# Banded attention and an ELU feed-forward layer on one core: rows of q and k spread by twos over 32 partitions

## The chip, the cores and the metric

The kernel runs on one NeuronCore of a Trainium2 chip, in one launch. The metric is the device time of a launch in microseconds. A core has five engines with a queue each, which work through their instructions in order and wait for each other through semaphores: TensorE (PE, matrix products), VectorE (DVE), ScalarE (ACT), GpSimd (POOL) and SyncE (SP, which here only issues DMAs). [...] All DMAs run on the same 16 DMA engines.

## The reference

```python
# q, k, v: [8 batches, 8 heads, 576, 64] float32; w_in [512, 2048], w_out [2048, 512]
scores = (q @ k.T) / sqrt(64)
rel    = i - j                                   # query row minus key row
mask   = (rel >= 0) & (rel < 128)
scores = where(mask, scores - slope[head] * abs(rel), -1e9)      # slope = 2 ** -(head + 1)
attn   = exp(scores - max) / sum
x      = (attn @ v) as [4608 tokens, 512]
h      = x @ w_in
out    = where(h > 0, h, exp(min(h, 0)) - 1) @ w_out             # [4608, 512] float32
```

A query row sees at most 128 keys, so that of the 576 x 576 scores of a head only a band is computed.

## The kernel before

**Layout of the attention.** A batch has 8 heads in four groups g of two, h2 = 0 and 1; group g has the partitions 32g to 32g+31. TensorE needs q and k with the 64 values of a row on the partitions, as two halves dh of 32. They come there in two steps. `load_qk(b, w, g)` (line 67) is a DMA of POOL that fetches two heads of q (w = 0) or k (w = 1), turns float32 into float16 and spreads the 576 rows over 32 partitions: partition i gets the 18 adjacent rows 18i to 18i+17 (R = 18), which lie behind one another in DRAM, 4,608 bytes a head. `turn_qk(b, w, h2, dh)` (line 74) then transposes on VectorE, in blocks of 32 x 32: for each r it takes 32 partitions by 32 values and writes a row of 32 values, one for each i, to the columns 18i + r of `QT` or `KT`. Its writes are thus 18 float16 values, 36 bytes, apart. A batch takes 8 loads and 8 transposes of 576 values per partition.

**The rest of the attention.** `scores` (line 145) multiplies on TensorE into one PSUM tile `sp`, four head groups side by side. ScalarE takes the exponential (`expo`, line 159), VectorE multiplies by a table `TAB` of bias and mask (`weigh`, line 162), TensorE multiplies by v with a column of ones (`values`, line 173; its PSUM tile `av` has one buffer), VectorE divides by the sum (line 188, 189). v comes by SP's DMAs (`load_v`, line 78, five tiles `vf`), and POOL casts it into `VP` (`cast_v`, line 83). `turn` brings the result to `xT`: by a DMA transpose, or for batch 0 by TensorE.

**The feed-forward layer** takes tokens in 9 blocks of 512, 16 steps each. `hidden` (line 213) makes a 128 x 512 tile `hp` on TensorE (two buffers), ScalarE takes its exponential into `e`, POOL clips it to at most 1, and `elu` (line 230) puts both together on VectorE into `g`, which frees `hp`. `output` (line 238) multiplies four chunks of `g` by `w_out`; after four such steps ScalarE copies the sum and SP stores it.

**The order of the work** is written out by hand, in slots (lines 257 to 357). A slot s issues, in this order: the early tasks (`before`, the exponentials), `hidden` of s, `elu` of s - 1, the tasks of `at(s, ...)`, `output`. Each engine takes its instructions in this order. Batch b > 0 starts at slot a = START[b] = 5, 21, 37, 55, 73, 91, 109: its loads are issued in the slots a-12 to a-5, one each (those of batch 1 before slot -5), its v loads from a-6 (batch 1: a-4), its transposes in a-4 to a+3, one each, its scores in a, a+4, a+8, a+12. Slots with a negative number are batch 0's first half, ahead of the first `hidden`. The transposes of batches 2 to 7 thus begin in the slots 17, 33, 51, 69, 87 and 105.

**The start.** POOL issues the 8 loads of batch 0, an iota for the table, the four weight loads `wi`, the 8 loads of batch 1, then the casts of v of batch 0. Its DMAs take turns on eight semaphores, so that an issue waits until the DMA eight places ahead of it has landed. SP issues v of batch 0 at once. `warm` (line 252) is a row of products of `ident` into a tile that nobody reads.

Of the kernel before, what the change touches and what calls it, by code (L numbers as in the profile page):

```python
# [7 lines left out]
F32 = mybir.dt.float32  # L8
F16 = mybir.dt.float16
# [9 lines left out]
def kernel(  # L19
# [9 lines left out]
    nc = tc.nc  # L29
    B, H, S, D = q.shape  # L30
    NTOK, DO = out.shape
# [2 lines left out]
    NTB = NTOK // 512  # L34
    RING = 3 * S
    VW = D + 2
    R = S // 32
    V = nc.vector

    const = ctx.enter_context(tc.tile_pool(name="const", bufs=1))  # L40
    stage = ctx.enter_context(tc.tile_pool(name="stage", bufs=2))
# [5 lines left out]
    ps_o = ctx.enter_context(tc.tile_pool(name="ps_o", bufs=1, space=PSUM))  # L47

    def one(shape, dt, name):
        return const.tile(shape, dt, name=name, tag=name)  # L50
# [5 lines left out]
    QT = [one([128, 2, 2, S], F16, f"QT{i}") for i in range(2)]  # L56
    KT = [one([128, 2, 2, 640], F16, f"KT{i}") for i in range(2)]
# [7 lines left out]
    st, vf = {}, {}  # L65

    def load_qk(b, w, g):
        if b not in st:
            st[b] = stage.tile([128, 2, 2, R, D], F16, name="st")
        nc.gpsimd.dma_start(  # L70
            st[b][32 * g:32 * g + 32, w, :, :, :].rearrange("p h r d -> p h (r d)"),
            (q, k)[w][b, 2 * g:2 * g + 2, :, :].rearrange("h (i r) d -> i h (r d)", r=R))

    def turn_qk(b, w, h2, dh):
        o = (QT, KT)[w][b % 2][:, h2, dh, 0:S].rearrange("p (i r) -> p r i", r=R)
        V.transpose(o, st[b][:, w, h2, :, 32 * dh:32 * dh + 32])  # L76

    def load_v(b, n):
        t = vf[b, n] = stage.tile([128, H, D], F32, name="vf", tag="vf", bufs=5)
        p = 128 if n < 4 else 64  # L80
        nc.sync.dma_start(t[0:p, :, :], v[b, :, 128 * n:128 * n + p, :].rearrange("h p d -> p h d"))

    def cast_v(b, n):
# [5 lines left out]
    def load_wi(i, n=1):  # L89
        c = slice(512 * i, 512 * i + 512 * n)  # L90
        nc.gpsimd.dma_start(w_in_sb[:, :, c], moe_w_in[:, c].rearrange("(c p) f -> p c f", p=128))
# [8 lines left out]
    with tc.manual_schedule():  # L100
# [7 lines left out]
        for g in range(4):  # L108
            load_qk(0, 1, g)
            load_qk(0, 0, g)  # L110
        for c, n in ((0, 256), (256, 192), (448, 64)):
            nc.gpsimd.iota(rel[:, c:c + n], pattern=[[1, n]], base=0, channel_multiplier=-1)
        load_wi(0)
        load_wi(1)
        for n in range(5):
            load_v(0, n)

        rowf = one([128, 1], F32, "rowf")
        V.tensor_copy(rowf, row)
# [127 lines left out]
                nc.scalar.copy(ob, ops[t])  # L247
                nc.sync.dma_start(out[512 * t + 128 * ts:512 * t + 128 * ts + 128, :], ob)

        spare = ps_o.tile([128, DO], F32, name="spare", tag="op")  # L250

        def warm(n):
            for _ in range(n):
                nc.tensor.matmul(spare[:, 0:128], ident, ident, start=True, stop=True)

# [3 lines left out]
        def at(s, f, *a):  # L259
            tasks.setdefault(s, []).append((f, a))  # L260
# [7 lines left out]
        START = [None, 5, 21, 37, 55, 73, 91, 109]  # L268


        warm(60)
        for h2 in range(2):
            for w in (1, 0):
                for dh in range(2):
                    at(-5 + h2, turn_qk, 0, w, h2, dh)
# [38 lines left out]
        for b in range(1, B):  # L314
            a = START[b]
            for k_ in range(4):
                u, h2 = divmod(k_, 2)
                at(a + 4 * k_, scores, b, k_)
                for g in range(4):
                    before(a + 4 * k_ + 1 + g, expo, b, k_, g)  # L320
                for gp in range(2):
                    at(a + 4 * k_ + 2 + 2 * gp, weigh, b, k_, gp)
                for n, i in enumerate((0, 1) if u == 0 else (2, 3, 4)):
                    at(a + 4 * k_ + 5 + n, values, b, i, h2)
                    if h2:
                        at(a + 4 * k_ + 5 + n, turn, b, i)
            order = [(w, h2, dh) for h2 in range(2) for w in (1, 0) for dh in range(2)]
            for n, what in enumerate(order):
                at(a - 4 + n, turn_qk, b, *what)
            for n in range(5):  # L330
                at(a - 6 + n if b > 1 else a - 4 + n, load_v, b, n)
                at(a - 2 + n, cast_v, b, n)
            if b > 1:
                for g in range(4):
                    for w in range(2):
                        at(a - 12 + 2 * g + w, load_qk, b, 1 - w, g)
# [51 lines left out]
```

## Time and profile before

| | us |
|---|---|
| median of 3 runs (lowest, highest) | 463.75 (462.43, 465.34) |
| the profiled execution, its own time | 464.51 |
| its span, first to last instruction | 462.2 |
| PE busy, share of the span | 338.5, 73% |
| DVE busy | 346.7, 75% |
| ACT busy | 176.9, 38% |
| POOL busy | 155.6, 34% |
| mean granted clock of TensorE | 0.882 |

A row of a group gives the line of the code, the engine, the operation and its tiles (out<-in), shapes as partitions x elements, the count; then busy time in us, the mean of one in ns, and how long the engine sat idle just before, with what ended the wait. [...] Busy times of engines overlap; those of one engine's instructions can overlap a little too.

### The profile page before, as it was taken

The page shows a single profiled execution, that of the slowest core. Times are in us where ns is not written, and L with a number is a line of the kernel's source. Part 1 is how long each engine was busy: PE and PEld are TensorE (multiplying, and loading weights), DVE is VectorE, ACT ScalarE, POOL GpSimd, SP SyncE. Part 2 cuts the span into 40 slices and gives each one's busy share as a digit, 9 for nine tenths or more (in the row PEclk, how much of TensorE's full clock was granted, in tenths as well). Part 3 has the DMA queues.
Part 4 walks back from the last instruction along what each step waited for, and adds up shares of the span by engine and source line. Part 5 has one row for each costly group of instructions (what it writes and reads, how often), then busy time and mean ns, then how long its engine had stood idle before and what let it go on. Part 6 is the DMA issues. An engine that isn't in the chain of part 4 may idle for free.

```text
span 462.2 us, 8158 instructions
## 1 busy us (share of the span) xinstructions
PE 338.5 (73%) x3280; PEld 226.8 (49%) x3280; DVE 346.7 (75%) x453; ACT 176.9 (38%) x317; POOL 155.6 (34%) x265
## 2 busy tenths in 40 slices
PE   4017467756697669987699468966698569999996
PEld 4006456533365345654366335643465346676652
DVE  3995998769867995699857997699867995674340
ACT  3122322513254234532256234533264234544441
POOL 7220532504143332523245223523263331333330
PEclk9555765979799797988889999999999897999999
DMA  9990750771249011961039211951069110211101
GB/s 172 199 208 1 107 90 13 90 151 34 54 81 181 23 28 37 143 144 24 29 62 186 62 42 35 155 131 28 24 115 183 40 36 7 64 45 53 47 23 68
DMA packets 69317, 37.16 MB, mean 80 GB/s; under 512 B 56480, under 2 KB 60576, under 8 KB 69280
## 3 DMA queue, kind: packets, MB, share of 16 engines
q0 software_dynamic: 9344, 13.64, 21.5%
q1 hardware_dynamic: 59936, 23.01, 19.7%
q8 instruction: 25, 0.41, 0.4%
q14 instruction: 12, 0.10, 0.1%
HBM read 36.70 MB, written 9.44 MB: 100 GB/s over the span
## 4 chain that ended last, share of the span: by engine, by line
DVE 44%; PE 37%; DMA 9%; issue 5%; ACT 3%; POOL 2%; DVEq 0%; ACTq 0%; POOLq 0%
PE op L243 18%; DVE QT L76 17%; PE hp L222 15%; DVE KT L76 14%; DMA st<-in_k_dram 7%; DVE g L234 6%; DVE EX L171 3%; DVE xn L189 3%; PE sp L154 3%; PE av L183 2%; DMA st<-in_q_dram 2%; ACT EX L160 1%; DVE rden L188 1%; ACT e L226 1%; POOL e L227 1%
## 5 line engine op out<-in xcount | busy, mean ns | idle before, releaser
L222 PE MATMUL hp<-xT,wi 128*128 128x256 f16 (+3 forms) x1408 | 163.7, 269 | 57.7 <-DVE g L234 57.7
L227 POOL TENSOR_SCALAR e<-e 128x512 f32<-128x512 f32 x144 | 90.9, 631 | 274.5 <-ACT e L226 274.5
L222 PEld LDWEIGHTS <-wi 128*128 128x128 f16 x1408 | 129.4, 106 | 109.0 <-issue 68.1
L226 ACT ACTIVATE e<-hp 128x512 f32<-128x512 f32 x144 | 86.1, 598 | 198.9 <-PE hp L222 198.9
L243 PE MATMUL op<-wo,g 128*128 128x512 f16 x576 | 157.3, 400 | 1.4 <-ACT ob L247 1.4
L234 DVE SCALAR_TENSOR_TENSOR g<-e,hp 128x512 f16<-128x512 f32 x144 | 108.5, 753 | 53.0 <-POOL e L227 53.0
L160 ACT ACTIVATE EX<-sp 128x512 f16<-128x512 f32 x128 | 75.2, 598 | 51.0 <-PE sp L154 50.7
L76 DVE STREAM_TRANSPOSE KT<-st 128x576 f16<-128x576 f16 x32 | 84.4, 2660 | 10.5 <-DMA st<-in_k_dram 10.3
L76 DVE STREAM_TRANSPOSE QT<-st 128x576 f16<-128x576 f16 x32 | 84.3, 2655 | 0.0
L243 PEld LDWEIGHTS <-g 128*128 128x128 f16 x576 | 51.3, 101 | 47.8 <-issue 13.1
L154 PE MATMUL sp<-QT,KT 32*128 32x256 f16 (+2 forms) x640 | 27.0, 284 | 48.1 <-DVE QT L76 43.4
L171 DVE TENSOR_TENSOR EX<-EX,TAB 128x1024 f16<-128x1024 f16 x64 | 48.1, 754 | 1.1 <-ACT EX L160 0.9
L154 PEld LDWEIGHTS <-KT 32*128 32x128 f16 x640 | 15.6, 99 | 57.7 <-issue 40.4
L183 PE MATMUL av<-VP,EX 128*128 128x65 f16 x576 | 33.7, 202 | 9.8 <-DVE xn L189 8.0
L188 DVE RECIPROCAL rden<-av 128x4 f32<-128x4 f32 x80 | 14.6, 182 | 30.1 <-PE av L183 29.2
L183 PEld LDWEIGHTS <-EX 128*128 128x128 f16 x576 | 29.8, 104 | 13.4 <-issue 5.2
L189 DVE TENSOR_TENSOR xn<-av,rden 128x256 f16<-128x256 f32 x80 | 34.0, 425 | 2.8
L247 ACT COPY ob<-op 128x512 f32<-128x512 f32 x36 | 21.1, 585 | 24.8 <-PE op L243 24.8
L85 POOL TENSOR_SCALAR VP<-vf 128x512 f16<-128x512 f32 (+1 forms) x40 | 24.5, 615 | 6.2 <-DMA vf<-in_v_dram 6.2
L70 POOL DMA_DIRECT2D st<-in_k_dram x32 | 18.3, 571 | 5.8 <-DMA wi<-in_moe_w_in_dram 5.1
L70 POOL DMA_DIRECT2D st<-in_q_dram x32 | 18.0, 563 | 5.3 <-DMA wi<-in_moe_w_in_dram 4.8
L135 ACT ACTIVATE TAB<-ra 128x512 f16<-128x512 f32 x8 | 4.3, 614 | 7.0 <-DVE ra L132 7.0
(25 smaller groups left out, 30.0 us busy)
## 6 DMA issues: line engine op xcount, KB each, us to landing
out_dram<-ob SPq DMA_DIRECT2D x36, 256.0 KB, 2.2
vf<-in_v_dram SPq DMA_DIRECT2D x32, 256.0 KB, 5.4
st<-in_k_dram POOLq DMA_DIRECT2D x32, 144.0 KB, 4.7
st<-in_q_dram POOLq DMA_DIRECT2D x32, 144.0 KB, 4.2
wi<-in_moe_w_in_dram POOLq DMA_DIRECT2D x4, 512.0 KB, 12.8
wo<-in_moe_w_out_dram POOLq DMA_DIRECT2D x4, 512.0 KB, 6.1
vf<-in_v_dram SPq DMA_DIRECT2D x8, 128.0 KB, 4.4
xT<-xn SPq DMA_TRANSPOSE x35, 2.4
```

What stands on the lines that cost most here:

```text
L70: nc.gpsimd.dma_start(st[b][32 * g:32 * g + 32, w, :, :, :].rearrange("p h r d -> p h (r d)"), (q, k)[w][b, 2 * g:2 * g + 2, :, :].rearran ...
L76: V.transpose(o, st[b][:, w, h2, :, 32 * dh:32 * dh + 32])
L154: nc.tensor.matmul(sp[:, g, o:o + n], kt[r, h2, dh, 128 * kb:128 * kb + 128], qt[r, h2, dh, q0:q0 + n], start=dh == 0, stop=dh == 1, tile_ ...
L160: nc.scalar.activation(unit(b, k_)[:, g, 0:512], sp[:, g, :], AF.Exp, scale=0.125)
L171: V.tensor_tensor(out=e, in0=e, in1=t, op=ALU.mult)
L183: nc.tensor.matmul(a[:, g, :], e[:, g, c:c + 128], VP[b % 2][:, n, 2 * g + h2, 0:D + 1], start=j == 0, stop=j == len(parts) - 1)
L189: V.tensor_tensor(out=xnt[b, i][:, :, h2, :], in0=a[:, :, 0:D], in1=r.unsqueeze(2).broadcast_to([128, 4, D]), op=ALU.mult)
L222: nc.tensor.matmul(p[:, l * w + u0:l * w + u1], w_in_sb[:, c, fc * 128:(fc + 1) * 128], xT[:, c, x0:x0 + u1 - u0], start=(c == 0), stop=(c ...
L226: nc.scalar.activation(e, p, AF.Exp)
L227: nc.gpsimd.tensor_scalar(out=e, in0=e, scalar1=1.0, scalar2=0.0, op0=ALU.min, op1=ALU.max)
L234: V.scalar_tensor_tensor(out=gs[t][:, f0:f0 + nf, c0:c0 + w], in0=sh(es.pop((t, j))), scalar=1.0, in1=sh(hps.pop((t, j))), op0=ALU.subtrac ...
L243: nc.tensor.matmul(ops[t], gs[t][:, fc, ts * 128:(ts + 1) * 128], w_out_sb[:, fc, :], start=(fc == 0), stop=(fc == NFC - 1))
```

## The change

- Row s of a head is now 64n + 2i + j, with n = 0 to 8, i = 0 to 31 and j = 0, 1: partition i gets rows by twos, nine pairs that lie 64 rows apart. A load moves 576 pieces of 512 bytes instead of 64 of 4,608.
- A transposed row of 32 values, one for each i, is written to the columns 64n + 2i + j: every 4 bytes instead of every 36. What is read, the number of transposes and their size stay.
- For batch 0, POOL writes one column of each v tile before SP may load it; in the code this stands behind the first weight load, and the second weight load follows it.
- `warm` takes a PSUM buffer of its own at each call, has 100 products instead of 60 at the beginning, and three more calls with 30 each in the slots -5, -4 and -3.

```diff
--- before.py
+++ after.py
@@ -34,7 +34,7 @@
     NTB = NTOK // 512
     RING = 3 * S
     VW = D + 2
-    R = S // 32
+    R = S // 64
     V = nc.vector
 
     const = ctx.enter_context(tc.tile_pool(name="const", bufs=1))
@@ -66,18 +66,20 @@
 
     def load_qk(b, w, g):
         if b not in st:
-            st[b] = stage.tile([128, 2, 2, R, D], F16, name="st")
+            st[b] = stage.tile([128, 2, 2, R, 2, D], F16, name="st")
         nc.gpsimd.dma_start(
-            st[b][32 * g:32 * g + 32, w, :, :, :].rearrange("p h r d -> p h (r d)"),
-            (q, k)[w][b, 2 * g:2 * g + 2, :, :].rearrange("h (i r) d -> i h (r d)", r=R))
+            st[b][32 * g:32 * g + 32, w, :, :, :, :].rearrange("p h n j d -> p (h n) (j d)"),
+            (q, k)[w][b, 2 * g:2 * g + 2, :, :].rearrange("h (n i j) d -> i (h n) (j d)", i=32, j=2))
 
     def turn_qk(b, w, h2, dh):
-        o = (QT, KT)[w][b % 2][:, h2, dh, 0:S].rearrange("p (i r) -> p r i", r=R)
-        V.transpose(o, st[b][:, w, h2, :, 32 * dh:32 * dh + 32])
+        o = (QT, KT)[w][b % 2][:, h2, dh, 0:S].rearrange("p (n i j) -> p n j i", i=32, j=2)
+        V.transpose(o, st[b][:, w, h2, :, :, 32 * dh:32 * dh + 32])
 
     def load_v(b, n):
         t = vf[b, n] = stage.tile([128, H, D], F32, name="vf", tag="vf", bufs=5)
         p = 128 if n < 4 else 64
+        if b == 0:
+            nc.gpsimd.memset(t[:, 0, 0:1], 0.0)
         nc.sync.dma_start(t[0:p, :, :], v[b, :, 128 * n:128 * n + p, :].rearrange("h p d -> p h d"))
 
     def cast_v(b, n):
@@ -111,9 +113,9 @@
         for c, n in ((0, 256), (256, 192), (448, 64)):
             nc.gpsimd.iota(rel[:, c:c + n], pattern=[[1, n]], base=0, channel_multiplier=-1)
         load_wi(0)
-        load_wi(1)
         for n in range(5):
             load_v(0, n)
+        load_wi(1)
 
         rowf = one([128, 1], F32, "rowf")
         V.tensor_copy(rowf, row)
@@ -247,9 +249,8 @@
                 nc.scalar.copy(ob, ops[t])
                 nc.sync.dma_start(out[512 * t + 128 * ts:512 * t + 128 * ts + 128, :], ob)
 
-        spare = ps_o.tile([128, DO], F32, name="spare", tag="op")
-
         def warm(n):
+            spare = ps_o.tile([128, DO], F32, name="spare", tag="op")
             for _ in range(n):
                 nc.tensor.matmul(spare[:, 0:128], ident, ident, start=True, stop=True)
 
@@ -268,7 +269,10 @@
         START = [None, 5, 21, 37, 55, 73, 91, 109]
 
 
-        warm(60)
+        warm(100)
+        at(-5, warm, 30)
+        at(-4, warm, 30)
+        at(-3, warm, 30)
         for h2 in range(2):
             for w in (1, 0):
                 for dh in range(2):
```

On POOL, at the start, where the loads of batch 0 end and the weights begin (`st` is the staged q or k, `wi` the first weight matrix, the numbers after DMASW one of POOL's eight semaphores). Before:

```order
L70 DMA st<-in_k_dram 32x2x1152
L70 DMA st<-in_q_dram 32x2x1152
L112 IOTA rel 128x256
L112 IOTA rel 128x192
L112 IOTA rel 128x64
L91 DMA wi<-in_moe_w_in_dram 128x4x512 [waits DMASW0_49]
L91 DMA wi<-in_moe_w_in_dram 128x4x512 [waits DMASW1_49]
```

And now:

```order
L70 DMA st<-in_k_dram 32x18x128
L70 DMA st<-in_q_dram 32x18x128
L114 IOTA rel 128x256
L114 IOTA rel 128x192
L114 IOTA rel 128x64
L93 DMA wi<-in_moe_w_in_dram 128x4x512 [waits DMASW0_49]
L82 MEMSET vf 128x1 x5
L93 DMA wi<-in_moe_w_in_dram 128x4x512 [waits DMASW1_49]
```

Five memsets have come between the first and the second weight load; the loads of q and k stand where they stood, in another shape.

Further on in POOL's queue, the last loads of batch 1 and the casts of batch 0's v (`vf` into `VP`), now:

```order
L70 DMA st<-in_k_dram 32x18x128 [waits DMASW2_49]
L70 DMA st<-in_q_dram 32x18x128 [waits DMASW3_49]
L87 TENSOR_SCALAR VP_85<-vf 128x8x64 [waits DMAHW0_49,Pool_49]
L87 TENSOR_SCALAR VP_85<-vf 128x8x64 [waits DMAHW1_49,Pool_49]
L87 TENSOR_SCALAR VP_85<-vf 128x8x64 [waits DMAHW2_49,Pool_49]
```

The casts still stand behind all of batch 1's loads, and these still wait for the weight loads; nothing has moved here.

On SP, the loads of v of batch 0, now:

```order
L83 DMA vf<-in_v_dram 128x8x64 [waits Pool_49] x4
L83 DMA vf<-in_v_dram 64x8x64 [waits Pool_49]
```

They stand first in SP's queue as before, where they waited for nothing; now they wait for POOL's memsets.

## Rows read from the trace of the kernel before

**Rows 1.** The page, busy time and its share of the span, by engine
```profile
PE 338.5 (73%) x3280; PEld 226.8 (49%) x3280; DVE 346.7 (75%) x453; ACT 176.9 (38%) x317; POOL 155.6 (34%) x265
```

**Rows 2.** The page, the chain that ended last, by engine and by line
```profile
DVE 44%; PE 37%; DMA 9%; issue 5%; ACT 3%; POOL 2%; DVEq 0%; ACTq 0%; POOLq 0%
PE op L243 18%; DVE QT L76 17%; PE hp L222 15%; DVE KT L76 14%; DMA st<-in_k_dram 7%; DVE g L234 6%; DVE EX L171 3%; DVE xn L189 3%; PE sp L154 3%; PE av L183 2%; DMA st<-in_q_dram 2%; ACT EX L160 1%; DVE rden L188 1%; ACT e L226 1%; POOL e L227 1%
```

**Rows 3.** Stretch, length, then busy PE, PEld, DVE, ACT, POOL, granted clock, DMA share, GB/s
```profile
40.50:96.10 55.60, 37.89 (x503) 31.39 (x500) 43.32 (x58) 21.93 (x40) 20.52 (x34) 0.74 0.51 71
96.10:353.60 257.50, 198.37 (x1884) 127.92 (x1885) 211.03 (x270) 104.16 (x189) 91.12 (x151) 0.92 0.43 82
252.50:281.00 28.50, 16.39 (x154) 10.17 (x153) 28.30 (x27) 8.81 (x16) 8.21 (x14) 1.00 0.25 67
281.00:303.00 22.00, 21.31 (x219) 14.89 (x218) 14.58 (x28) 12.35 (x23) 10.30 (x18) 1.00 0.71 118
353.60:382.00 28.40, 17.10 (x195) 10.88 (x191) 28.19 (x27) 8.49 (x15) 7.79 (x13) 0.91 0.24 65
400.00:462.20 62.20, 56.78 (x429) 36.53 (x426) 24.96 (x43) 24.00 (x42) 16.61 (x28) 1.00 0.14 48
```

**Rows 4.** Groups by line in 252.5 to 281: busy us, mean ns | idle before
```profile
L76 DVE STREAM_TRANSPOSE KT<-st 128x576 f16<-128x576 f16 x4 | 10.6, 2643 | 0.1
L234 DVE SCALAR_TENSOR_TENSOR g<-e,hp 128x512 f16<-128x512 f32 x8 | 7.0, 872 | 0.0
L171 DVE TENSOR_TENSOR EX<-EX,TAB 128x1024 f16<-128x1024 f16 x3 | 2.0, 661 | 0.0
L189 DVE TENSOR_TENSOR xn<-av,rden 128x256 f16<-128x256 f32 x4 | 1.7, 425 | 0.1
L188 DVE RECIPROCAL rden<-av 128x4 f32<-128x4 f32 x4 | 0.7, 168 | 0.0
```

**Rows 5.** Groups by line and form, whole run: the transposes, two DVE rows, POOL's DMA issues
```profile
L76 DVE STREAM_TRANSPOSE KT<-st 128x576 f16<-128x576 f16 x32 | 84.4, 2660 | 10.5 <-DMA st<-in_k_dram 10.3
L129 DVE TENSOR_TENSOR ra<-ra,rel 128x512 f32<-128x512 f32 x1 | 0.7, 693 | 0.0
L123 DVE MEMSET VP<- 128x40 f16 x2 | 0.2, 92 | 0.2
L70 POOL DMA_DIRECT2D st<-in_k_dram x32 | 18.3, 571 | 5.8 <-DMA wi<-in_moe_w_in_dram 5.1 <-DMA st<-in_k_dram 0.3 <-issue 0.3
L91 POOL DMA_DIRECT2D wi<-in_moe_w_in_dram x4 | 3.0, 750 | 1.5 <-DMA st<-in_k_dram 1.0 <-DMA st<-in_q_dram 0.4
```

**Rows 6.** Timeline of the start: start, length, engine, line, idle before
```profile
1.62 5.09 PE L254 MATMUL spare<-ident 128*128 128x128 f16 x60 [1.62 <-DVE ident L120]
12.61 5.10 DVE L76 STREAM_TRANSPOSE KT<-st 128x576 f16<-128x576 f16 x2 [3.65 <-DMA st<-in_k_dram]
25.57 0.53 POOL L70 DMA_DIRECT2D st<-in_q_dram  x1 [1.99 <-DMA wi<-in_moe_w_in_dram]
26.13 2.36 POOL L85 TENSOR_SCALAR VP<-vf 128x512 f16<-128x512 f32 x4
33.30 0.64 PE L183 MATMUL av<-VP,EX 128*128 128x65 f16 x4
40.52 1.91 PE L222 MATMUL hp<-xT,wi 128*128 128x128 f16 x16
```

**Rows 7.** The page, DMA queues over the run: packets, MB, share of 16 engines
```profile
q0 software_dynamic: 9344, 13.64, 21.5%
```

**Rows 8.** DMA queues in 0 to 12: packets, MB, share of 16 engines
```profile
q1 hardware_dynamic: 3505, 0.89, 35.1%
```

**Rows 9.** DMA queues in 80 to 90
```profile
q0 software_dynamic: 335, 0.62, 48.9%
```

**Rows 10.** DMA queues in 42 to 60
```profile
q0 software_dynamic: 1450, 1.45, 55.6%
```

**Rows 11.** Timeline of VectorE where batch 2's first transpose starts
```profile
96.11 2.64 DVE L76 STREAM_TRANSPOSE KT<-st 128x576 f16<-128x576 f16 x1 [3.52 <-DMA st<-in_k_dram]
```

## The prediction

> **What bounds the kernel now.** I read the page's totals first, then the chain of waits, then busy time by stretch, then the groups of one stretch. In the totals no engine is full: VectorE has 75% and TensorE 73% [rows 1]. The chain says that the two take turns: VectorE carries 44% of it, TensorE 37%, and the lines that stand out are the two transposes of line 76 with 31% together [rows 2]. The stretches show the turns. From 252.5 to 281 us, the eight slots in which batch 5's q and k are transposed, VectorE is busy for 28.30 of 28.5 us and TensorE for 16.39. From 281 to 303, the next ten slots, TensorE is busy for 21.31 of 22 us and VectorE for 14.58 [rows 3]. So a batch costs about 28.5 + 22 = 50.5 us, the first part set by VectorE and the second by TensorE. In the first part the eight transposes hold 21.1 us (four of k at 10.6, four of q alike), the rest 11.4 us of durations: g 7.0, weighing 2.0, xn 1.7, reciprocals 0.7 [rows 4]. These records overlap a little, since 28.30 is less than their sum; without the transposes VectorE has between 28.30 - 21.1 = 7.2 and 11.4 us to do there. The last 62.2 us hold no transposes [rows 3].
>
> **The transposes.** 64 of them, 2.66 us for 576 values per partition [rows 5], 4.6 ns a value. The input is read in the same runs of 32 values; only the step of the writes changes, from 36 bytes to 4. No transpose with another step is in this trace. The bounds come from other VectorE rows. Below: line 129 writes one 4-byte value after another, so every 4 bytes, at 693 ns for 512 values [rows 5], 1.35 ns each; 576 of these are 0.78 us. Above, if a small step helps at all: the memset of line 123 writes 40 values 132 bytes apart in 92 ns [rows 5], 2.3 ns each or 1.32 us for 576; and if the step does not matter, the 2.66 us stay. I take 0.78, because line 129 is the row with exactly the new step. The memset speaks against me in part: its writes lie further apart than today's transposed ones and cost half as much, so the step alone may not explain 4.6 ns.
>
> [...]
>
> **What that is worth, stage by stage** (462.2 us of span, 464.5 as timed in the profiled execution; the median is 463.75, 0.75 less).
> - *Batches 2 to 6, 96.1 to 353.6 us*, 88 slots, 257.5 us [rows 3]. The eight transposing slots: VectorE has 7.2 to 11.4 us plus 8 x 0.78 = 6.2, so 13.4 to 17.6; TensorE has its 16.39. The two come level; I take 18 us instead of 28.5. The other ten slots stay at 22, since TensorE fills them. That makes 40 us for a batch of 18 slots; one of the five has 16 slots, two of the 2-us kind fewer, 36. Sum 4 x 40 + 36 = 196, **61.5 us less**.
> - *Batch 7's transposes*, 28.4 us with VectorE busy for 28.19 [rows 3]: 18 instead, **10.4 less**. The 80 us behind them I leave as they are.
> - *Batch 1, 40.5 to 96.1*, 55.6 us: VectorE is busy for 43.32 and would be for 43.3 - 8 x 1.88 = 28.3. [...] I take 38, TensorE's own time, **17.6 less**.
> - *The start, 0 to 40.5.* Batch 0's eight transposes run from 12.61 to about 32.5, the first values at 33.30, the first hidden product at 40.52 [rows 6]. Eight short ones would be done by 19 us, 13 us earlier. But the values also need VP, and POOL casts v at 26.13, right after the last of its load issues, which sat behind a landing weight load until 25.57 [rows 6]. That order stays, so only 33.3 - 26.7 = 6.6 us can be had. Of this the smaller packets (below) take up to 3.3 us, for twelve loads ahead of the cast; I keep **5 less**.
>
> **The loads of q and k.** 64 loads go from 64 packets of 4,608 bytes to 576 of 512 bytes. *On POOL*: an issue of 64 packets takes 571 ns, one of 512 takes 750 [rows 5], 0.4 ns a packet, so 0.2 us more each, 13 us in all. POOL is busy for 34% [rows 1], and each slot of 2 us holds one issue and one 0.6-us operation on e: hidden by POOL's idle time. Were POOL full, it would be 13 us. *On the DMA engines*: the queue's 9,344 packets [rows 7] are 64 x 64 + 8 x 512 of data and 1,152 others, 16 for each DMA. In 80 to 90 us it carried q and k alone, 335 packets in 48.9% of 160 engine-us [rows 9], 234 ns a packet, or 292 for each data packet if the small ones are free. By bytes 512 of them cost 32 ns. The v loads' packets of 256 bytes cost 35.1% of 192 engine-us over 3,505, 19 ns [rows 8]; the weights' of 2,048 cost 55.6% of 288 over 1,450, 110 ns [rows 10]. So a new packet lies between 19 and 110 ns. I take 40, near the byte rate and twice the v packet: 576 x 40 / 16 engines = 1.44 us a load against 1.17. One load is issued per slot of 2.2 us, so they still fit; twelve at the start add 3.3 us, taken off above. The first transpose of a batch already waits for its k load now and then, 3.52 us at the worst [rows 11]; 0.3 us more of that is inside my rounding of 17.6 to 18.
>
> [...]
>
> **The small edits, together.** v of batch 0 now waits for POOL's memsets, five of about 0.1 us, behind the first weight load. It leaves the engines to q and k in the first 9 us, which may bring the first transpose forward by 2 us, off the path since the cast decides. v then has from 9 to 29 us to land; if it were later than that, the start would grow by what it is late. The added products of ident: 60 took 5.09 us [rows 6], so 130 end near 12.7 us, before the first transposes are done; the two later sets of 30, 2.5 to 5 us each, stand in the stretch in which TensorE waits for the cast. Cost nothing; without that cover, 10 us.
>
> **Sum**: -61.5 - 10.4 - 17.6 - 5 = -94.5. 464.5 - 94.5 = 370.0, by the median **369 us**.
>
> **Rivals.**
> 1. *Transposes of 1.32 us*, the memset's price. For it: that row is a write with a step. Against: its step is 132 bytes. A transposing stretch has 17.8 to 22 us of VectorE, I take 21: 3 more, six times, and 4 in batch 1: **391 us**. Chance 0.14.
> 2. *Packets at twice the byte rate*, 64 ns: 2.3 us a load, a little over a slot. Each of six batches is late by 8 x 0.1 us, and the start by 8 x 1.1: **383**. Chance 0.07.
> 3. *The step does not set the price*: transposes stay at 2.66 us. For it the memset row, against it nothing in the trace. VectorE bounds the same stretches, the start gains at most 2 us and loses 1: **463**. Chance 0.09.
> 4. *Slower: a packet costs what a weight packet does*, 110 ns, whatever its bytes. A load then takes 4.0 us, and the eight are issued 2.2 us apart; the first transposes of six batches come 8 x 1.8 = 14 us late and the start 8 x 2.8 = 22 later, 108 in all. With the gain this is 477; it decides from about 104 ns, where 48 x (0.036 p - 2.2) + 8 x (0.036 p - 1.17) eats up 94.5. Against it: 19 ns for 256 bytes. Time **477**, chance 0.04.
>
> **The numbers.** The forecast has 0.66. Its own range is 345 to 385: below, if the eight slots run at TensorE's 16.4 (10 us), batch 1 takes 32 at a better clock (6), the start gives all 6.6 (1.6), and batches 2 to 6, at a mean clock of 0.92 [rows 3], win back half of 0.08 x 198 (8); above, at 2.5 us more per transposing stretch. With rivals 1 and 2 the range is 345 to 398 and holds 0.66 x 0.9 + 0.14 + 0.07 = 0.8. A measurement of this kernel can tell about 1%. Faster by more: 0.66 + 0.14 + 0.07 = 0.87. Within 1%: rival 3, 0.09. Slower: 0.04.
>
> **What would show it.** The transpose rows at 0.7 to 0.9 us; at 1.3 rival 1 is right, at 2.6 rival 3. TensorE above 88% of the span, and its waits for g in the transposing slots nearly gone. The first values near 29 us, behind the cast of v. The q0 packets: 42,112, at about 40 ns. I am wrong if the idle time before the first transpose of each batch grows to several us (the loads), if the hidden products still wait for g although VectorE is not full (the way from hidden product through ScalarE and POOL back to VectorE being too long), or if the cast of v slips past 33 us.

## The result, and the profile after

The changed kernel takes **353.08 us** (median of 4 runs, 352.23 to 353.57) against 464.54 (4 runs, 462.43 to 466.15): a ratio of 0.760, with an interval of 0.756 to 0.764. Forecast were 369 us, with a range of 345 to 398. The span of the profiled execution went from 462.2 to 350.9 us, 111.3 less, where the sum had 94.5. Slow executions, among them ones of 553, 824 and 1,241 us, are left out of the ratios.

Line numbers of the kernel after are two higher than before from line 81 on, and four at the end. First the page of the kernel after: the totals, the chain by engine, and POOL's DMA queue. They answer to [rows 1, 2, 7].

```profile
PE 314.4 (90%) x3410; PEld 221.1 (63%) x3410; DVE 236.6 (67%) x453; ACT 176.3 (50%) x317; POOL 169.6 (48%) x270
PE 71%; DVE 8%; DMA 8%; issue 4%; ACT 4%; POOL 3%; ACTq 0%; DVEq 0%; POOLq 0%
q0 software_dynamic: 42112, 13.64, 36.6%
```

VectorE's share of the chain has fallen from 44% to 8%, TensorE's has grown from 37% to 71%, and TensorE is busy for 90% of the span. The queue has the 42,112 packets that were worked out. Their price: 36.6% of 350.9 us on 16 engines are 2,055 engine-us; less 4,096 weight packets at the 110 ns that they took in the kernel before [rows 10], 1,604 remain for 36,864 packets, 44 ns each (forecast: 40).

The groups by line and form over the whole run, to set beside [rows 5], and the start, to set beside [rows 6] (start, length, engine, line, idle before):

```profile
L76 DVE STREAM_TRANSPOSE KT<-st 128x576 f16<-128x576 f16 x32 | 25.9, 817 | 3.4 <-DMA st<-in_k_dram 3.3
L70 POOL DMA_DIRECT2D st<-in_k_dram x32 | 22.1, 690 | 6.1 <-DMA wi<-in_moe_w_in_dram 5.6 <-issue 0.5
```

```profile
1.62 10.22 PE L255 MATMUL spare<-ident 128*128 128x128 f16 x130 [1.62 <-DVE ident L122]
11.16 1.50 DVE L76 STREAM_TRANSPOSE KT<-st 128x576 f16<-128x576 f16 x2 [0.94 <-DMA st<-in_k_dram]
26.31 0.66 POOL L70 DMA_DIRECT2D st<-in_q_dram  x1 [2.70 <-DMA wi<-in_moe_w_in_dram]
26.99 1.21 POOL L87 TENSOR_SCALAR VP<-vf 128x512 f16<-128x512 f32 x2
27.68 0.38 PE L185 MATMUL av<-VP,EX 128*128 128x65 f16 x4 [8.54 <-POOL VP L87]
34.89 1.91 PE L224 MATMUL hp<-xT,wi 128*128 128x128 f16 x16
```

A transpose takes 0.82 us instead of 2.66, forecast were 0.78. An issue on POOL has grown from 571 to 690 ns, 0.12 us instead of the 0.2 that were allowed. At the start the transposes run from 11.16 us, but the values wait for the cast of v, which stands behind the last load issue as it did: first values at 27.68 instead of 33.30, first hidden product at 34.89 instead of 40.52.

Busy time by stretch, in the columns of [rows 3]: batch 1; batches 2 to 6; the eight transposing slots of batch 5 and the ten slots behind them; batch 7's transposing slots; the rest.

```profile
34.90:73.90 39.00, 30.27 (x496) 24.63 (x495) 29.32 (x59) 21.02 (x39) 22.32 (x34) 0.92 0.88 124
73.90:257.90 184.00, 179.05 (x1886) 122.19 (x1883) 142.59 (x271) 104.58 (x190) 100.14 (x151) 1.00 0.71 116
183.60:198.40 14.80, 14.29 (x138) 9.64 (x139) 13.95 (x27) 8.05 (x15) 7.85 (x13) 1.00 0.46 104
198.40:221.40 23.00, 22.31 (x239) 15.46 (x238) 15.14 (x28) 13.00 (x24) 11.84 (x19) 1.00 0.81 126
257.90:272.50 14.60, 14.44 (x184) 10.50 (x183) 13.69 (x26) 7.80 (x15) 8.10 (x13) 1.00 0.47 109
272.50:350.90 78.40, 72.43 (x600) 47.45 (x599) 35.42 (x63) 33.24 (x59) 21.48 (x35) 1.00 0.16 49
```

Transposing slots and the others now look alike. In the eight slots from 183.6 us both engines are nearly full, TensorE for 14.29 and VectorE for 13.95 of 14.8 us; in the ten behind them TensorE is, for 22.31 of 23.0. The granted clock, a share of full speed, had a mean of 0.74 in batch 1 and 0.92 in batches 2 to 6 [rows 3]; now it is 0.92 and then 1.00. The groups of those eight slots answer to [rows 4]. First TensorE's groups in the same slots before, which [rows 4] does not have, and then now:

```profile
L222 PE MATMUL hp<-xT,wi 128*128 128x256 f16 x60 | 7.8, 272 | 9.2 <-DVE g L234 9.2
L243 PE MATMUL op<-wo,g 128*128 128x512 f16 x30 | 7.8, 380 | 0.0
L154 PE MATMUL sp<-QT,KT 32*128 32x256 f16 x32 | 1.6, 272 | 2.9 <-DVE QT L76 2.9
```

```profile
L224 PE MATMUL hp<-xT,wi 128*128 128x256 f16 x58 | 7.6, 272 | 0.2 <-DVE g L236 0.2
L245 PE MATMUL op<-wo,g 128*128 128x512 f16 x28 | 7.2, 379 | 0.0
L156 PE MATMUL sp<-QT,KT 32*128 32x256 f16 x20 | 0.9, 271 | 0.3 <-ACT EX L162 0.3
L236 DVE SCALAR_TENSOR_TENSOR g<-e,hp 128x512 f16<-128x512 f32 x8 | 5.2, 653 | 0.3 <-POOL e L229 0.3
L76 DVE STREAM_TRANSPOSE KT<-st 128x576 f16<-128x576 f16 x4 | 3.3, 822 | 0.3 <-DMA st<-in_k_dram 0.3
L173 DVE TENSOR_TENSOR EX<-EX,TAB 128x1024 f16<-128x1024 f16 x3 | 2.0, 679 | 0.0
L191 DVE TENSOR_TENSOR xn<-av,rden 128x256 f16<-128x256 f32 x4 | 1.7, 425 | 0.1
L190 DVE RECIPROCAL rden<-av 128x4 f32<-128x4 f32 x4 | 0.7, 172 | 0.4 <-PE av L185 0.4
```

TensorE hardly waits for g any longer: 0.2 us of idle time ahead of the hidden products instead of 9.2. g itself has become shorter, 653 ns instead of 872; why was not tried. A product takes as long as before, but fewer of them fall into these slots: 58, 28 and 20 here, where 60, 30 and 32 stood.

| stretch | before, us | after, us | less by | forecast |
|---|---|---|---|---|
| start, to the first hidden product | 40.5 | 34.9 | 5.6 | 5 |
| batch 1, to batch 2's first transpose | 55.6 | 39.0 | 16.6 | 17.6 |
| batches 2 to 6 | 257.5 | 184.0 | 73.5 | 61.5 |
| batch 7's transposing slots | 28.4 | 14.6 | 13.8 | 10.4 |
| the rest | 80.2 | 78.4 | 1.8 | 0 |

### The profile page after: what moved, and what is told of

It reads as the page before. It is cut to its first block, busy times and chain, and to the rows that moved or that the text cites. A ratio compares the mean times of both kernels' runs of the same rounds, so it can differ in the third digit from the quotient of the medians.

```text
span 350.9 us, 8428 instructions
## 1 busy us (share of the span) xinstructions
PE 314.4 (90%) x3410; PEld 221.1 (63%) x3410; DVE 236.6 (67%) x453; ACT 176.3 (50%) x317; POOL 169.6 (48%) x270
## 3 DMA queue, kind: packets, MB, share of 16 engines
q0 software_dynamic: 42112, 13.64, 36.6%
## 4 chain that ended last, share of the span: by engine, by line
PE 71%; DVE 8%; DMA 8%; issue 4%; ACT 4%; POOL 3%; ACTq 0%; DVEq 0%; POOLq 0%
PE op L245 32%; PE hp L224 30%; PE sp L156 5%; PE av L185 4%; DMA st<-in_k_dram 4%; DMA wi<-in_moe_w_in_dram 4%; ACT EX L162 3%; DVE g L236 2%; DVE EX L173 2%; POOL st L70 2%; DVE xn L191 1%; DVE KT L76 1%; DVE QT L76 1%; ACT ob L249 1%; POOL e L229 1%
## 5 line engine op out<-in xcount | busy, mean ns | idle before, releaser
L229 POOL TENSOR_SCALAR e<-e 128x512 f32<-128x512 f32 x144 | 95.7, 665 | 147.7 <-ACT e L228 147.2
L224 PE MATMUL hp<-xT,wi 128*128 128x256 f16 (+3 forms) x1408 | 151.5, 255 | 7.1 <-DVE g L236 6.5
L224 PEld LDWEIGHTS <-wi 128*128 128x128 f16 x1408 | 120.1, 99 | 49.0 <-issue 11.5
L245 PE MATMUL op<-wo,g 128*128 128x512 f16 x576 | 146.7, 379 | 1.4 <-ACT ob L249 1.4
L236 DVE SCALAR_TENSOR_TENSOR g<-e,hp 128x512 f16<-128x512 f32 x144 | 96.8, 672 | 57.3 <-POOL e L229 57.1
L76 DVE STREAM_TRANSPOSE KT<-st 128x576 f16<-128x576 f16 x32 | 25.9, 817 | 3.4 <-DMA st<-in_k_dram 3.3
L156 PE MATMUL sp<-QT,KT 32*128 32x256 f16 (+2 forms) x640 | 21.1, 255 | 7.8 <-ACT EX L162 5.4
L76 DVE STREAM_TRANSPOSE QT<-st 128x576 f16<-128x576 f16 x32 | 25.7, 811 | 0.0
L70 POOL DMA_DIRECT2D st<-in_k_dram x32 | 22.1, 690 | 6.1 <-DMA wi<-in_moe_w_in_dram 5.6
L156 PEld LDWEIGHTS <-KT 32*128 32x128 f16 x640 | 15.2, 95 | 13.8 <-issue 11.6
L255 PE MATMUL spare<-ident 128*128 128x128 f16 x190 | 13.9, 244 | 1.7 <-DVE ident L122 1.6
```

Source lines behind the costliest of these rows:

```text
L70: nc.gpsimd.dma_start(st[b][32 * g:32 * g + 32, w, :, :, :, :].rearrange("p h n j d -> p (h n) (j d)"), (q, k)[w][b, 2 * g:2 * g + 2, :, : ...
L76: V.transpose(o, st[b][:, w, h2, :, :, 32 * dh:32 * dh + 32])
L156: nc.tensor.matmul(sp[:, g, o:o + n], kt[r, h2, dh, 128 * kb:128 * kb + 128], qt[r, h2, dh, q0:q0 + n], start=dh == 0, stop=dh == 1, tile_ ...
L224: nc.tensor.matmul(p[:, l * w + u0:l * w + u1], w_in_sb[:, c, fc * 128:(fc + 1) * 128], xT[:, c, x0:x0 + u1 - u0], start=(c == 0), stop=(c ...
L229: nc.gpsimd.tensor_scalar(out=e, in0=e, scalar1=1.0, scalar2=0.0, op0=ALU.min, op1=ALU.max)
L236: V.scalar_tensor_tensor(out=gs[t][:, f0:f0 + nf, c0:c0 + w], in0=sh(es.pop((t, j))), scalar=1.0, in1=sh(hps.pop((t, j))), op0=ALU.subtrac ...
```

## The experiments

Each shows a short diff against the changed kernel unless it says otherwise, and ratios are to the kernel before in the same job.

### One part at a time

**The layout alone.**

```diff
-        if b == 0:
-            nc.gpsimd.memset(t[:, 0, 0:1], 0.0)
...
-        warm(100)
-        at(-5, warm, 30)
...
+        warm(60)
```

> The changed kernel without its small edits: v of batch 0 loaded at once and 60 products of ident, as before; rows spread by twos stay. Theory A (the step of the transposed writes makes the gain): transposes stay at 0.82 us, and the time at 353 to 358 us, since the first values still wait for the cast of v near 27 us. Theory B (a good part of the 111 us comes from the small edits: q and k alone on the DMA engines at the start, a warm TensorE): 365 us or more.

353.57 us, ratio 0.761 (0.756 to 0.766): theory A. The small edits are worth nothing that a measurement of this kernel can tell. The first values come at 27.45 us with them left out, at 27.68 with them in.

**The small edits alone**, put into the kernel before (the same lines, added).

> The kernel before with the small edits alone: v of batch 0 behind POOL's memsets, 100 and three times 30 products of ident; rows as before, writes 36 bytes apart. Theory A: transposes stay at 2.66 us, the first transpose starts up to 2 us earlier, and the time is 461 to 466 us. Theory B: 455 us or less.

465.05 us (eight runs), ratio 1.001 (0.997 to 1.006): no effect, as theory A had it.

**The step of the writes alone**: the loads of before.

```diff
-            st[b][32 * g:32 * g + 32, w, :, :, :, :].rearrange("p h n j d -> p (h n) (j d)"),
-            (q, k)[w][b, 2 * g:2 * g + 2, :, :].rearrange("h (n i j) d -> i (h n) (j d)", i=32, j=2))
+            st[b][32 * g:32 * g + 32, w, :, :, :, :].rearrange("p h n j d -> p h (n j d)"),
+            (q, k)[w][b, 2 * g:2 * g + 2, :, :].rearrange("h (i r) d -> i h (r d)", r=18))
```

> The changed kernel with the loads of before (64 packets of 4,608 bytes, 18 adjacent rows to a partition) and the new step of the transposed writes, so that the rows of q and k land in permuted columns and another attention is computed. Theory A: the transposes cost 0.82 us here too; packets of 40 ns instead of 292 for nine times the bytes were worth 3.3 us at the start and nothing later, so 349 to 352 us. Theory C (the small packets cost more than that, hidden in slots that could run faster): 345 us or less. If the transposes need the new spread of the rows to be fast: 2.66 us each and 460 us.

Transposes of 818 ns, and 357.86 us (355.13 to 359.87), ratio 0.770 (0.764 to 0.776). The main point holds: the step makes the transposes fast, not the spread of the rows. But theory A's time was missed: the large packets are no better than the small ones, and 4.8 us worse by the medians, with intervals that just touch. The start did win 1.5 us (first values at 26.13), and lost it again by batch 2, whose first transpose waits longer for k. VectorE's row there, with the large packets and then in the changed kernel:

```profile
75.29 0.81 DVE L76 STREAM_TRANSPOSE KT<-st 128x576 f16<-128x576 f16 x1 [3.25 <-DMA st<-in_k_dram]
```

```profile
73.88 0.83 DVE L76 STREAM_TRANSPOSE KT<-st 128x576 f16<-128x576 f16 x1 [0.90 <-DMA st<-in_k_dram]
```

3.25 us of idle time against 0.90; from batch 2 on such waits are 6.3 us against 2.4. The profiled execution was the fastest of the four, 355.13 us, and its span is 2.3 us longer than the changed kernel's, so it shows only a part of the 4.8. That the waits make the loss is a reading; why k lands later there was not tried.

**The packets alone**: writes 36 bytes apart again.

```diff
-        o = ...rearrange("p (n i j) -> p n j i", i=32, j=2)
+        o = ...rearrange("p (i n j) -> p n j i", n=R, j=2)
```

> The changed kernel with its loads (576 packets of 512 bytes) but the transposed writes 36 bytes apart as before; rows land in permuted columns, another attention is computed. Theory A: transposes back at 2.66 us and the time at 460 to 466 us. Theory C (small packets cost more): above 468 us. If the spread of the rows and not the step makes the transposes fast: 0.82 us and 353 us.

Transposes of 2,659 ns and 463.21 us, ratio 0.996 (0.993 to 1.000). Nine times the packets in each load cost nothing where VectorE sets the pace; theory C falls.

### The step, from 2 to 18 bytes

The spread by twos becomes one by J rows, J = 1, 3, 6, 9, with the loads and the writes to match; for J = 3:

```diff
-    R = S // 64
+    R = S // 96
...
-            st[b] = stage.tile([128, 2, 2, R, 2, D], F16, name="st")
+            st[b] = stage.tile([128, 2, 2, R, 3, D], F16, name="st")
...
-        o = ...rearrange("p (n i j) -> p n j i", i=32, j=2)
+        o = ...rearrange("p (n i j) -> p n j i", i=32, j=3)
```

> Rows one by one over 32 partitions (18 rows 32 apart): transposed writes 2 bytes apart, packets of 256 bytes, 1,152 a load. Line theory (a write pays when it opens a new 16-byte line): transposes at 0.75 to 0.82 us, no gain over 4 bytes. Theory of a price that grows in proportion to the step (0.82 us at 4 bytes, 2.66 at 36, so 0.0575 us a byte): 0.71 us. Packets: at 19 to 30 ns each a load takes 1.4 to 2.2 us, so the time is 352 to 360 us.

> Rows by threes: writes 6 bytes apart, packets of 768 bytes, 384 a load. Line theory: 0.82 us if two or more writes to a line are free, 1.13 if each new line pays in proportion (0.375 of the writes open one). Proportional theory: 0.94 us. Time 349 to 358 us.

> Rows by sixes: writes 12 bytes apart, packets of 1,536 bytes. Line theory: three of four writes open a new line, so about 2.0 us a transpose. Proportional theory: 1.28 us. Time 415 to 430 us by the first, 370 to 390 by the second.

> Rows by nines: writes 18 bytes apart, packets of 2,304 bytes. Line theory: every write opens a new line, as at 36 bytes: 2.66 us and 460 us. Proportional theory: 1.63 us and 390 to 405 us.

The groups by line and form, the transposes of k in each of the four (those of q are alike), 2, 6, 12 and 18 bytes in this order; the mean in ns is the number behind the comma:

```profile
L76 DVE STREAM_TRANSPOSE KT<-st 128x576 f16<-128x576 f16 x32 | 24.4, 767 | 10.4 <-DMA st<-in_k_dram 10.4
```

```profile
L76 DVE STREAM_TRANSPOSE KT<-st 128x576 f16<-128x576 f16 x32 | 36.1, 1137 | 5.4 <-DMA st<-in_k_dram 5.4
```

```profile
L76 DVE STREAM_TRANSPOSE KT<-st 128x576 f16<-128x576 f16 x32 | 67.0, 2112 | 5.8 <-DMA st<-in_k_dram 5.8
```

```profile
L76 DVE STREAM_TRANSPOSE KT<-st 128x576 f16<-128x576 f16 x32 | 86.9, 2740 | 6.6 <-DMA st<-in_k_dram 6.6
```

| step, bytes | packet, bytes | writes that open a new 16-byte line | ns a transpose | time, us | ratio (interval) |
|---|---|---|---|---|---|
| 2 | 256 | 72 of 576 | 767 | 359.11 | 0.774 (0.771 to 0.777) |
| 4 (the change) | 512 | 144 | 817 | 353.08 | 0.760 (0.756 to 0.764) |
| 6 | 768 | 216 | 1,137 | 364.31 | 0.785 (0.782 to 0.788) |
| 12 | 1,536 | 432 | 2,112 | 424.27 | 0.914 (0.910 to 0.917) |
| 18 | 2,304 | 576 | 2,740 | 468.85 | 1.012 (1.005 to 1.019) |
| 36 (before) | 4,608 | 576 | 2,660 | 464.54 | 1 |

The line theory holds, in its form without a free second hit: from 4 bytes up each further new line costs (1,137 - 817) / 72 = 4.4 ns, then (2,112 - 1,137) / 216 = 4.5 ns and (2,740 - 2,112) / 144 = 4.4 ns, and 18 bytes cost no less than 36. At 6 bytes a line takes 2.67 writes, and the transpose still costs 1.14 us and not 0.82. The 16 bytes were the theory's; the rows put the end of the rise near there: from 4 to 12 bytes a byte of step costs (2,112 - 817) / 8 = 162 ns, and at that rate the 2,660 ns of 36 bytes and the 2,740 of 18 are reached at 15.4 and 15.9 bytes. A line is thus a reading of these six prices; nothing else here shows one. The proportional theory had 1.28 us at 12 bytes and 1.63 at 18, and is out. At 2 bytes the transposes stay near 0.77 us, where 72 lines fewer would have saved 0.3: a floor. Of the whole times two fall outside what was expected by the line theory: 364.31 us at 6 bytes (349 to 358) and 468.85 at 18 (460). The rows at 12 and 18 bytes rest on two and three runs. Of the steps tried 4 bytes is the best: 2 bytes save 0.05 us a transpose and take packets of 256 bytes, with which the waits for k are 10.4 us in all instead of 3.3, and the kernel is 6 us slower. That it is slower because of these waits was not tried by itself.

### Strided writes by themselves

The tile `scr` and a dense source `dense`, itself filled by a memset just ahead, are set up in lines left out here.

```diff
+        for step in (18, 9, 3, 2, 1):
+            part = scr[:, 0:576 * step].rearrange("p (n s) -> p n s", s=step)[:, :, 0]
+            V.memset(part, 1.0)
+            V.tensor_copy(part, dense)
```

> The changed kernel with ten extra VectorE instructions ahead of batch 0's transposes: a memset and a copy of 576 float16 values each, written 36, 18, 6, 4 and 2 bytes apart, into a tile nobody reads. Theory W (the price is one of strided writes, 4.4 ns for each new 16-byte line): both operations cost about 2.7 us at 36 and 18 bytes, 1.1 at 6, at most 0.8 at 4 and 2. Theory T (the price belongs to the transpose alone): memset and copy cost 0.65 to 0.8 us at every step, as the memset row of 40 values 132 bytes apart in 92 ns suggests.

The timeline of VectorE, where each pair stands in the order 36, 18, 6, 4, 2 bytes; the idle time of an instruction is in brackets, `issue` where the profile shows nothing that it waited for:

```profile
12.78 0.54 DVE L147 MEMSET scr<- 128x576 f16 x1 [1.94 <-issue]
13.35 1.40 DVE L148 COPY scr<-dense 128x576 f16<-128x576 f16 x1
16.85 0.54 DVE L147 MEMSET scr<- 128x576 f16 x1 [2.10 <-issue]
17.43 1.42 DVE L148 COPY scr<-dense 128x576 f16<-128x576 f16 x1
19.39 0.54 DVE L147 MEMSET scr<- 128x576 f16 x1 [0.54 <-DVE scr L148]
19.96 0.65 DVE L148 COPY scr<-dense 128x576 f16<-128x576 f16 x1
20.83 0.54 DVE L147 MEMSET scr<- 128x576 f16 x1 [0.23 <-DVE scr L148]
21.41 0.49 DVE L148 COPY scr<-dense 128x576 f16<-128x576 f16 x1
22.08 0.54 DVE L147 MEMSET scr<- 128x576 f16 x1 [0.19 <-DVE scr L148]
22.65 0.36 DVE L148 COPY scr<-dense 128x576 f16<-128x576 f16 x1
```

The memset's record is 0.54 us at every step, which is theory T, and would make the memset no measure of a write's price. But the idle time ahead of each is not the same: idle and record together are 2.48, 2.64, 1.08, 0.77 and 0.73 us, near the transposes' 2.66, 2.74, 1.14, 0.82 and 0.77. The first stands behind a dense memset of another tile, so its 1.94 us are not the end of a strided write in front. And behind the copies at 36 and 18 bytes, which are alike (1.40 and 1.42 us), stand 2.10 and 0.54 us: the idle time goes with the step of the memset that follows (18 and 6 bytes), not with the copy's. So I read that idle time as the memset's own, and theory W as right for it. This is a reading and not shown: each step was run once, and the two small memsets of [rows 5], 132 bytes apart, have 0.08 and 0.09 us of idle time in front, no more than the dense ones beside them. The copies pay about half: 1.40, 1.42, 0.65, 0.49 and 0.36 us, (1.40 - 0.65) / 360 = 2.1 ns for a new line. Why half was not tried. The kernel with these ten instructions ran once, in 360.48 us.

### The start

POOL casts v ahead of batch 1's loads, the second unit is weighed ahead of the first values; the small edits are left out.

```diff
         for n in range(4):
             at(-4, cast_v, 0, n)
-        at(-3, values, 0, 0, 0)
-        at(-3, values, 0, 1, 0)
+        for g in range(4):
+            for w in (1, 0):
+                at(-4, load_qk, 1, w, g)
...
         at(-3, weigh, 0, 1, 1)
+        at(-3, values, 0, 0, 0)
+        at(-3, values, 0, 1, 0)
...
-        for g in range(4):
-            for w in (1, 0):
-                load_qk(1, w, g)
```

> The changed layout without the small edits (v at once, 60 products), and POOL casts v of batch 0 ahead of batch 1's loads, VectorE weighs the second unit ahead of the first values. Theory A (the place of the casts in POOL's queue sets the start): the first values start at 20 to 23 us instead of 27.7, the first hidden product at 27 to 30 instead of 34.9, and the time is 346 to 350 us. Theory D (the DMA engines bound the start, whatever the order): batch 1's first transpose waits for its k rows until 34 us or later, the first slots stand still for it, and the time is 352 to 355 us.

351.05 us, ratio 0.756 (0.752 to 0.759), where the change has 0.760 (0.756 to 0.764): not told apart. Both theories are right by half. Timeline of the start, from an execution of 354.81 us, the slowest of seven: POOL's casts, the first values, the first hidden product, batch 1's first transpose.

```profile
13.41 2.37 POOL L85 TENSOR_SCALAR VP<-vf 128x512 f16<-128x512 f32 x4
22.59 0.40 PE L183 MATMUL av<-VP,EX 128*128 128x65 f16 x4
30.90 1.91 PE L222 MATMUL hp<-xT,wi 128*128 128x128 f16 x16
39.15 0.81 DVE L76 STREAM_TRANSPOSE KT<-st 128x576 f16<-128x576 f16 x1 [3.50 <-DMA st<-in_k_dram]
```

The cast was the brake: values come 5.1 us earlier, hidden products 4.0. Then batch 1's first transpose waits for its k until 39.15 us, where the changed kernel has it at 39.55, and in this execution the gain is given back.

Two runs after that hold back v of batch 1 (`if b == 1` in place of `if b == 0` at its memset), the second one also starts batch 1 in slot 7 instead of 5.

> The start order of the run before (casts of v of batch 0 ahead of batch 1's loads, second unit weighed ahead of the first values), and v of batch 1 held back by a POOL memset in its slot, so that batch 1's q and k have the DMA engines to themselves after the weights. Theory E (v of batch 1 took the DMA time from batch 1's k): batch 1's first transpose starts by 36 us instead of 39.15, the time is 346 to 349 us. Theory D (the DMA engines bound the start by the bytes that must come, whatever the order): first transpose at 38 us or later, 350 to 353 us.

> The same with batch 1 started two slots later (START 7 instead of 5), so that its first transpose stands in slot 3. Theory E: little more to gain, 345 to 349 us. Theory D: two slots of about 2 us come ahead of the wait, so that up to 3 us are won against the run above: 347 to 350 us.

354.20 us, ratio 0.762 (0.759 to 0.766), and 358.38, ratio 0.774 (0.769 to 0.778). In the first, the part on k is right and the time wrong:

```profile
30.11 1.91 PE L224 MATMUL hp<-xT,wi 128*128 128x128 f16 x16
34.77 0.82 DVE L76 STREAM_TRANSPOSE KT<-st 128x576 f16<-128x576 f16 x1
```

The first transpose comes at 34.77 us, 4.4 us earlier than in the run before, and still batch 2 starts at 72.85 us against 73.88 in the changed kernel. Of 4.8 us won at the first hidden product, 1.0 us is left in the profile and nothing in the times. The later start of batch 1 is worse. What slows batch 1's slots then stays open in part. From the first hidden product to batch 2's first transpose TensorE was granted a mean clock of 0.84 in the run before these and 0.87 in the first of them, where the changed kernel has 0.92, and its products took 33.8 and 31.9 us instead of 30.3, while the stretch is 5.0 and 3.8 us longer. All three runs on the start leave out the added products of `warm`. So does the layout alone, and over its whole span it has a clock of 0.956, where the changed kernel has 0.969 to 0.976 and the first two runs on the start 0.950 to 0.956. Whether the missing products lower the clock of batch 1's slots is not shown: the new order with those products was not run. No kernel here beats the change by more than the measurement tells.

## Why the prediction was right

- *The transposes*, 0.82 us for a forecast of 0.78: right, and for the reason given, the step of the writes. That line 129 came so near is partly luck: it is another operation on 4-byte values that lie densely, and nothing showed that its 1.35 ns were a price of its writes. The rival of the memset's price, 1.32 us, came from a row that could not show one: in the run with strided writes a memset's record is 0.54 us at every step.
- *Batches 2 to 6 and batch 7* carry the miss of 16.8 us in the sum: 15.4 us more was won there than forecast. The term that was sized wrong is "I take 18 us" for a transposing stretch. From the first transpose to the g behind the last, the five stretches of batches 2 to 6 take 15.3, 17.1, 14.8, 14.7 and 14.7 us, 76.6 where the forecast has 90; batch 7's takes 14.6 for 18; the other slots of batches 2 to 6 take 107.4 for 106.
- *Why 18 was too much*: it is VectorE's upper end, 17.6, rounded up. That end adds up durations that overlap. The lower one, with the measured 0.82, is 7.2 + 8 x 0.82 = 13.8, and 13.95 is what VectorE took. TensorE's 16.39 was a little too much as well, mostly because the stretch then held other products: 154, with 18.8 us of durations, against 138 with 17.3 now (1.6 of them in both are the products with v). The ones that are missing stand in the ten slots behind, which have 239 instead of 219 and take 23.0 us instead of 22.0. Over the 18 slots TensorE was busy for 16.39 + 21.31 = 37.7 us before [rows 3], and they take 14.8 + 23.0 = 37.8 now: for this batch its busy time over all 18 slots was the bound, and the forecast's 40 lay above it.
- *The clock* stands in the prediction's range only, as 8 us more that batches 2 to 6 might win and 6 more in batch 1. But batch 5, from which the 22 us were taken, had a granted clock of 1.00 already, while these batches together had 0.92 [rows 3]: to take 22 for all of them was to forecast the higher clock for all. It came. TensorE's busy time there fell from 198.4 to 179.1 us for the same number of products, and the slots without transposes became 8.0 us shorter in all (115.4 to 107.4), where the prediction has them stay.
- *The start*: 5.6 for 5, set by the cast of v as argued; moving the casts confirmed it.
- *Batch 1*: 16.6 for 17.6, but by luck. The forecast took 38 us as TensorE's own time, the 37.89 of [rows 3]. TensorE was busy for 30.3 us there, at a clock of 0.92 instead of 0.74, and VectorE for 29.3 of 39.0; neither is full, and hidden products still waited 5.1 us for g. That is one of the signs of being wrong that the prediction lists, and in this stretch it is there. The 32 us "at a better clock" of the prediction's range no run shows: the stretch took 39.0, at 0.92.
- *The packets*: 44 ns for 40; packets alone cost nothing. By the byte rate of before a new packet would take 32 ns, so that 44 are 12 more and not the 64 of rival 2; what makes the 12 was not shown. The 3.3 us that smaller packets were to take from the start were 1.5 by the run with large ones, and the large ones lost more than that later. Rivals 2 and 4 are out; rival 3 is what 18 bytes look like.
- *The small edits*: nothing, as costed.

## What to carry to other kernels

Look at the bytes between successive writes of a VectorE instruction: here a transpose took 0.82 us at a step of 4 bytes, 1.14 at 6, 2.11 at 12 and 2.66 at 36, and the way rows were dealt to partitions when they were loaded chose that step. When one engine's work shrinks, take the other's need over a whole period of the schedule, here a batch of 18 slots, and not over a part of it: instructions move between the parts. A sum of durations that exceeds the stretch's busy time is too high as a need. And look at the granted clock of the stretch that a forecast is taken from before you scale it to others.

## What the runs showed of the hardware

- A VectorE transpose of 576 float16 values takes 0.77 us when it writes densely, 0.82 at a step of 4 bytes, 1.14 at 6, 2.11 at 12, 2.74 at 18 and 2.66 at 36. Between 4 and 18 bytes that is 4.4 to 4.5 ns for each further write that opens a new 16-byte line, counted as in the table.
- A memset's record has one length, 0.54 us for 576 values, at steps from 2 to 36 bytes, while the idle time in front of it is 0.19 us at 2 bytes, 2.10 at 18 and 1.94 at 36; whether that time is the memset's own is not shown.
- A DMA issue on POOL costs 571 ns for 64 packets, 690 for 576 and 840 for 1,152, about 0.25 ns a packet.
- A DMA packet of q or k, float32 to float16, took 44 ns for 512 bytes read and 278 for 4,608, which is 0.086 and 0.060 ns a byte. These are estimates: the first is worked out above, the second in the same way from 9,344 packets at 21.5% [rows 7], 1,590 engine-us, less 451 for the weights, over 4,096 packets.
